# Attention in front of two feed-forward stages: one burst of scores in the last sequence, and normalising taken off GpSimd

## The chip, the cores and the metric

The kernel runs on one core of a Trainium2 chip. The metric is the device time of one execution in microseconds (us), from which comparisons are made over several runs. A core has five engines with instruction queues of their own: PE (TensorE, matrix products into the eight banks of PSUM), DVE (VectorE), ACT (ScalarE), POOL (GpSimd) and SP, which issues loads and stores.

## The reference, cut to what matters

Three stages, all in float32. Attention over 4 sequences of 576 tokens with 8 heads of width 64, a window of 128 tokens and a bias by distance; then a feed-forward stage of width 2048 with a low-rank mixing over tokens; then a gated stage.

```
scores = scale * q @ k^T ;  scores = where(mask, scores + bias, -1e9)
attn   = exp(scores - max) / (sum + 1e-9) ;  x = attn @ v
u = x + (x^T @ U @ V)^T                      # low rank, over tokens
y = u + relu(u @ w_ch1) @ w_ch2              # 512 -> 2048 -> 512
h = relu(y @ w_in) ; ... ; out = (gate) @ w_out
```

The inputs are q, k, v, U, V, w_ch1, w_ch2, w_in, w_spatial, b_spatial and w_out; the output is 4 x 576 x 512.

## The kernel before, in words

Work is written down as tasks (`P.add`, `P.either`) with an engine, a cost in us and what they read and write. A planner (`Plan.run`) then orders all tasks of the whole kernel in list scheduling: it goes forward in time, gives each engine the ready task of the best priority, then sets priorities from the end backward, eight times, and emits the order with the shortest planned time. So a change of one task's engine or cost can move the order of everything up to where the plans meet again. A task given to POOL, or to DVE with `port=True`, also excludes the other of these two in the plan. On the chip each engine runs its instructions in the order emitted and waits by semaphores.

Attention goes by *pairs*: two heads of one sequence, four pairs per sequence, 16 in all. The 576 queries of a pair are nine tiles of 64; tile t needs up to 192 keys. `heads(b, pair)` does:

- L1033, scores: for each tile two matmuls, one per head, in quarters of 64x64 of the PE array, into PSUM tiles named `sc`. `TILES` cuts the nine tiles into six and three, so a pair has one piece of 12 matmul instructions and one of 6 (the trace records each of them as two: 24 and 12). The very first pair has three pieces.
- L1044 on DVE: adds the bias, writes `p`, takes the row maximum (a second small instruction reads it out). L1049 on ACT: exponential with row sums.
- L1055, L1057 on DVE: `rinv`, the inverse of the row sums.
- In sequence 0 (`plain`), L1060 on POOL spreads `rinv` into diagonal blocks `dg` (tiles `y`), L1090 on PE turns these into factors over rows, and L1124 multiplies at the end. In sequences 1 to 3, L1069 on POOL or L1071 on DVE multiplies each tile of `p` by `rinv`; the planner chooses the engine for each tile.
- L1079 on PE: 13 transposes of `p` in four groups (3, 3, 3, 4) into PSUM tiles `at`; L416 (ACT) or L417 (DVE) copies each group out to `ph`.
- L1117 on PE: weighted sums, 32 instructions (64 in the trace); copies to `u`.

`turned` transposes `u` (L1144), and `low_rank` does the mixing (L1160 and L1173 on PE, L1178 on DVE). Weight conversion for the feed-forward stage (L452 on ACT, L458, L459, L462, L465 on DVE, L603 on POOL) runs beside attention, and so do three blocks of 512 tokens of the feed-forward stage: L545 to L547 first layer, L584 to L586 second layer, with L529 (ACT) and L532 (POOL) splitting `u`. These have a later priority and fill PE where attention waits. The next stage on PE starts with L545 on tiles of 384 columns.

PSUM tiles come from rings of banks: `sc` three, `at` three, `acc` one, `f1` one. Sequence 0 uses `acc` and `f1` as well, since nothing else needs them yet. A ring gives its banks in turn, so a new tile waits for the last reader of the bank's former tile.

Of the kernel before, what the change touches and what calls it, by code (L numbers as in the profile page):

```python
# [333 lines left out]
def pool_tt(n):  # L334
    return 0.0021 * n + 0.15
# [3 lines left out]
def tile_kernel(ctx, tc, qT, kT, v, U, V, w1, w2, w_in, wspT, bsp, w_out, bias, out):  # L339
    nc = tc.nc  # L340
# [63 lines left out]
    r_at0 = Ring(in_psum, "at", 3, more=["f1_0"])  # L404
    r_f4 = Ring(in_psum, "at", 3, more=["f1_0"])
    r_a4 = Ring(in_psum, "sc", 3, more=["acc_0"])

    ident = left.tile([128, 128], F32, tag="ident", name="ident")
    make_identity(nc, ident)
# [577 lines left out]
    def heads(b, pair):  # L987
# [1 line left out]
        i = b * H + pair * 2  # L989
        p0 = 10.0 * i  # L990
        hs = slice(pair * 2, pair * 2 + 2)
        sc, tp = (r_sc0, r_at0) if b == 0 else (r_sc, r_at)
        qr, kr = r_qr.new([128, S], F32), r_kr.new([128, S], F32)

        vr = r_vr.new([128, 2, 4, D], F32)
        groups = TILES
        if i:
            for t, src in ((qr, qT), (kr, kT)):
                P.dma(128, S, lambda t=t, src=src: nc.sync.dma_start(out=t.ap(), in_=src[b, hs].rearrange("h d s -> (h d) s")),
# [54 lines left out]
        def rest():  # L1054
# [2 lines left out]
            P.add("DVE", 0.105, lambda: nc.vector.reciprocal(out=rinv[:, sl, :9], in_=rinv[:, sl, :9]), w=[rinv.part(sl)], prio=p0 + 4)  # L1057
            if plain:
                dg = r_d.new([128, 9, D], F32)
                P.add("POOL", pool_tt(S), lambda: nc.gpsimd.tensor_tensor(  # L1060
                    out=dg.ap(), in0=eye.ap().broadcast_to([128, 9, D]),
                    in1=rinv[:, sl, :9].rearrange("p (t o) -> p t o", o=1).broadcast_to([128, 9, D]), op=ALU.mult),
                    r=[rinv.part(sl), eye.part(0), eye.part(1)], w=[dg], prio=p0 + 4)
            else:
                for t in range(9):
                    nk = 64 * min(t + 1, 3)
                    o = lambda t=t, nk=nk: p[:, AT[t] : AT[t] + nk]
                    P.either([
                        ("POOL", pool_tt(nk), lambda o=o, t=t, nk=nk: nc.gpsimd.tensor_tensor(  # L1069
                            out=o(), in0=o(), in1=rinv[:, sl, t : t + 1].broadcast_to([128, nk]), op=ALU.mult)),  # L1070
                        ("DVE", dve2(nk) + 0.06, lambda o=o, t=t: nc.vector.tensor_scalar_mul(  # L1071
                            out=o(), in0=o(), scalar1=rinv[:, sl, t : t + 1])),
                    ], r=[rinv.part(sl)], w=[p.part(t)], prio=p0 + 4 + t / 10, port=True)
# [58 lines left out]
    def turned(b, half):  # L1132

        p0 = 10.0 * (b * H + half * 4 + 3)
        tp = r_at0 if b == 0 else r_at
        xt = r_xt.new([128, 5, 2, 128], F32)
        for c0 in (0, 2, 4):
            cs = range(c0, min(c0 + 2, 5))
            x = tp.new([128, len(cs), 2, 128], F32)
            for i in range(2):  # L1140
                ub = u[b][half * 2 + i]
                for c in cs:

                    P.add("PE", 0.109, lambda x=x, c=c, c0=c0, i=i, ub=ub: nc.tensor.transpose(  # L1144
                        x[:, c - c0, i], ub[:, TOK[c][0] : TOK[c][0] + 128], ident),
                        r=[ub.part(0), ub.part(1)], w=[x], prio=p0 + 8.5)
            copy(engines("h", "ACT"), 256 * len(cs), lambda c0=c0, cs=cs: xt[:, c0 : c0 + len(cs)], x.ap, PSUM,
                 r=[x], w=[xt.part(c0)], prio=p0 + 8.6)
        return xt

    def low_rank(b, xts, pairs, p0):

        sc, tp = (r_sc0, r_at0) if b == 0 else (r_sc, r_at)
        rows = slice(pairs[0] * 32, pairs[-1] * 32 + 32)
        t, th = tp.new([128, 128], F32), r_th.new([128, 128], F32)

        def mix():
            for c in range(5):
                for pair in pairs:
                    nc.tensor.matmul(t[pair * 32 : pair * 32 + 32], u32[:, c], xts[pair // 2][:, c, pair % 2],  # L1160
                                     start=c == 0, stop=c == 4, skip_group_check=True)

        P.add("PE", 5 * 4 * 128 / 2400 + 0.1, mix, r=[u32] + [xts[h].part(c) for h in {p // 2 for p in pairs} for c in (0, 2, 4)],
              w=[t], prio=p0, mode="quarters")
        copy(engines("t", "ACT"), 128, lambda: th[rows], lambda: t[rows], PSUM, r=[t], w=[th], prio=p0 + 0.05)
        for s0 in (0, 288):
            sl = slice(s0, s0 + 288)
            outs = [(sc, tp)[pair % 2].new([128, 288], F32) for pair in pairs]

            def up(sl=sl, outs=outs):  # L1170
                for pair, o in zip(pairs, outs):
                    d = slice(pair * 32, pair * 32 + 32)
                    nc.tensor.matmul(o.ap(), th[d], v32[d, sl], start=True, stop=True)  # L1173

            P.add("PE", 4 * 288 / 2400 + 0.1, up, r=[th] + list(v32.parts.values()), w=outs, prio=p0 + 0.1, mode="quarter rows")
            for pair, o in zip(pairs, outs):
                ub = u[b][pair]
                P.add("DVE", dve(288), lambda o=o, ub=ub, sl=sl: nc.vector.tensor_tensor(  # L1178
                    out=ub[:, sl], in0=o.ap(), in1=ub[:, sl], op=ALU.add),
                    r=[o], w=[ub.part(0), ub.part(1), ub], prio=p0 + 0.2)  # L1180
# [544 lines left out]
```

## Time and profile before

| what | value |
|---|---|
| median of 3 runs | 715.44 us (715.12 to 715.75) |
| the profiled execution | 715.53 us |
| its span, first to last instruction | 713.7 us |
| mean granted TensorE clock | 0.999 |
| PE busy | 700.3 us (98%) |
| DVE busy | 575.2 us (81%) |
| ACT busy | 395.3 us (55%) |
| POOL busy | 68.5 us (10%) |

Attention and what runs beside it fill the first 190 us or so. In the profile busy times come from recorded starts and modelled ends: matmuls are pipelined, so that a matmul of 0.4 us may start 0.23 us after the one ahead of it. The distance of two starts tells more than a duration there. Line numbers below are those of the kernel before; in the changed kernel the same lines stand 1 to 3 further down.

### The profile page before, as it was taken

What the parts mean: (1) busy time and instruction counts of PE and PEld (TensorE: products, weight loads), DVE (VectorE), ACT (ScalarE), POOL (GpSimd) and SP (SyncE); (2) the same over time, 40 slices, a digit from 0 to 9 for tenths busy, and PEclk for the clock granted to TensorE, in tenths of its full rate; (3) what the DMA queues carried; (4) which work ended last, traced back from release to release, by engine and by line L of the source; (5) the groups of instructions that cost most, each with busy time, mean ns of one, the idle gap of its engine ahead of it and who ended that gap; (6) DMA issues with size and microseconds to landing.
All of it is one profiled execution on the core that took longest, in us unless ns stands there. A gap on an engine that the chain in (4) does not pass through costs nothing.

```text
span 713.7 us, 14785 instructions
## 1 busy us (share of the span) xinstructions
PE 700.3 (98%) x5416; PEld 635.7 (89%) x5416; DVE 575.2 (81%) x1641; ACT 395.3 (55%) x1087; POOL 68.5 (10%) x104
## 2 busy tenths in 40 slices
PE   7999999999999999999999999999999999999998
PEld 4767677778799999999999999999999898898896
DVE  5999997775497999999694999697589989859561
ACT  6878576565353745546262563544257566566352
POOL 2142330210400000000000000030010100100000
PEclk9999999999999999999999999999999999999999
DMA  8774212210064165637565455457795202100102
GB/s 258 230 248 148 73 51 83 74 51 2 1 201 158 59 232 204 229 109 244 177 205 194 152 202 192 128 166 240 256 382 181 77 33 68 48 26 1 60 1 75
DMA packets 58798, 98.48 MB, mean 138 GB/s; under 512 B 8356, under 2 KB 38308, under 8 KB 58725
## 3 DMA queue, kind: packets, MB, share of 16 engines
q1 hardware_dynamic: 58437, 97.23, 41.3%
q8 instruction: 43, 0.70, 0.4%
q10 hardware_dynamic: 288, 0.30, 0.1%
q14 instruction: 30, 0.25, 0.1%
HBM read 67.67 MB, written 29.54 MB: 136 GB/s over the span
## 4 chain that ended last, share of the span: by engine, by line
PE 92%; DVE 6%; DMA 1%; issue 1%; ACT 0%; POOL 0%; SPq 0%; DVEq 0%
PE sc L586 8%; PE sc L584 8%; PE sc L585 8%; PE at L885 6%; PE at L886 6%; PE at L887 6%; PE at L1117 4%; PE sc L1033 3%; PE at L1079 3%; PE sc L1412 2%; PE sc L1411 2%; PE sc L1410 2%; PE acc L584 2%; PE at L1412 2%; PE at L1410 2%; PE at L1411 2%
## 5 line engine op out<-in xcount | busy, mean ns | idle before, releaser
L584 PE MATMUL sc<-h,wa 128*128 128x384 f32 (+1 forms) x328 | 110.6, 337 | 0.0
L585 PE MATMUL sc<-h,wa 128*128 128x384 f32 (+1 forms) x328 | 110.5, 337 | 0.0
L586 PE MATMUL sc<-hl,wa 128*128 128x384 f32 x320 | 108.7, 340 | 0.0
L1049 ACT ACTIVATE p<-p,nmax 128x192 f32<-128x192 f32 (+2 forms) x144 | 61.4, 430 | 11.5 <-DVE nmax L1044 11.2
L584 PEld LDWEIGHTS sc<-h,wa 128*128 128x128 f32 x328 | 61.6, 188 | 0.3
L585 PEld LDWEIGHTS sc<-h,wa 128*128 128x128 f32 x328 | 61.5, 187 | 0.3
L885 PE MATMUL at<-xd,wa 128*128 128x384 f32 x180 | 60.9, 338 | 0.0
L886 PE MATMUL at<-xd,wa 128*128 128x384 f32 x180 | 60.8, 338 | 0.0
L887 PE MATMUL at<-xd,wa 128*128 128x384 f32 x180 | 60.8, 338 | 0.0
L586 PEld LDWEIGHTS sc<-hl,wa 128*128 128x128 f32 x320 | 60.1, 188 | 0.0
L933 DVE TENSOR_TENSOR y<-sc,y 128x384 f32<-128x384 f32 (+1 forms) x96 | 40.3, 448 | 20.4 <-PE sc L586 20.2
L1044 DVE CUSTOM_DVE_ANT_0 p<-sc,bias 128x192 f32<-128x192 f32 (+2 forms) x144 | 40.8, 326 | 15.8 <-PE sc L1033 15.6
L905 ACT COPY c<-at 128x384 f32<-128x384 f32 x54 | 25.8, 477 | 42.2 <-PE at L887 42.0
L416 ACT CAST wa<-st 128x256 fp32r<-128x256 f32 (+1 forms) x62 | 27.9, 474 | 26.5 <-DVE st L465 14.2
L897 ACT ACTIVATE h<-c 128x384 fp32r<-128x384 f32 x54 | 28.3, 524 | 19.1 <-DVE c L892 18.9
L1033 PE MATMUL sc<-kr,qr 64*64 64x192 f32 (+2 forms) x576 | 33.3, 328 | 5.3 <-DMA kr<-in_kT 3.3
L892 DVE TENSOR_TENSOR c<-at,c 128x384 f32<-128x384 f32 x54 | 29.7, 551 | 8.3 <-PE at L887 4.7
L885 PEld LDWEIGHTS at<-xd,wa 128*128 128x128 f32 x180 | 33.8, 188 | 0.0
L886 PEld LDWEIGHTS at<-xd,wa 128*128 128x128 f32 x180 | 33.8, 188 | 0.0
L887 PEld LDWEIGHTS at<-xd,wa 128*128 128x128 f32 x180 | 33.8, 188 | 0.0
L1079 PE MATMUL at<-ident,p 128*128 128x128 f32 x208 | 30.9, 284 | 2.5 <-DVE p L1071 1.6
L1079 PEld LDWEIGHTS at<-ident,p 128*128 128x128 f32 x208 | 22.9, 142 | 11.5 <-issue 2.8
(404 smaller groups left out, 1996.5 us busy)
## 6 DMA issues: line engine op xcount, KB each, us to landing
wa<-in_w SPq DMA_DIRECT2D x32, 512.0 KB, 4.4
xd<-formsa SPq DMA_DIRECT2D x24, 192.0 KB, 3.3
qr<-in_qT SPq DMA_DIRECT2D x15, 288.0 KB, 2.9
kr<-in_kT SPq DMA_DIRECT2D x15, 288.0 KB, 3.3
vr<-in_v SPq DMA_DIRECT2D x16, 256.0 KB, 3.3
raw<-in_w_in SPq DMA_DIRECT2D x8, 512.0 KB, 4.0
kepts<-raw SPq DMA_DIRECT2D x14, 288.0 KB, 2.7
out<-h SPq DMA_DIRECT2D x15, 256.0 KB, 2.0
```

The lines of the kernel that those rows point to most:

```text
L584: nc.tensor.matmul(o, wt[:, 0, 0, c], hh[:, j], start=i == 0 and x == 0, stop=False, skip_group_check=True)
L585: nc.tensor.matmul(o, wt[:, 1, 0, c], hh[:, j], start=False, stop=False, skip_group_check=True)
L586: nc.tensor.matmul(o, wt[:, 0, 0, c], hl[:, j], start=False, stop=i == len(wts) - 1, skip_group_check=True)
L885: nc.tensor.matmul(o.ap(), wh()[:, k], xh.ap(), start=start and k == 0, stop=False, skip_group_check=True)
L886: nc.tensor.matmul(o.ap(), wl()[:, k], xh.ap(), start=False, stop=False, skip_group_check=True)
L887: nc.tensor.matmul(o.ap(), wh()[:, k], xl.ap(), start=False, stop=k == 1, skip_group_check=True)
L892: P.add("DVE", dve(N3), lambda: nc.vector.tensor_tensor(out=out.ap(), in0=ps_.ap(), in1=sb.ap(), op=ALU.add), r=[ps_, sb], w=[out], prio=0)
L933: P.add("DVE", dve(m), lambda acc=acc, dst=dst, s=s, m=m, o=o: nc.vector.tensor_tensor(out=dst[:, s : s + m], in0=acc[:, 0, o : o + m], in ...
L1033: nc.tensor.matmul(s[o : o + 64, c0 : c0 + k1 - k0], qr[d, 64 * t : 64 * t + 64], kr[d, k0:k1], start=True, stop=True, skip_group_check=True)
L1044: nc.vector.tensor_tensor_reduce(out=o(), in0=s[:, c0 : c0 + nk], in1=bias_t[:, pair, t % 2, 192 - nk :], scale=-0.125, scalar=BIG, op0=AL ...
L1049: nc.scalar.activation(out=o(), in_=o(), func=AF.Exp, scale=-1.0, bias=nmax[:, sl, t : t + 1], accum_out=sums[:, sl, t : t + 1])
L1079: P.add("PE", 0.109, lambda pt=pt, n_=n_, s0=s0: nc.tensor.transpose(pt[:, n_ - s0], p[:, n_ * 128 : n_ * 128 + 128], ident), r=[p.part(t) ...
```

## The change

A new ring `r_sc1` holds the three `sc` banks and the third `at` bank, and `r_at1` the two `at` banks that are left. The last sequence (b = 3) uses them for scores, transposes, weighted sums, turning and low rank, and issues all nine score tiles of a pair as one task. The diagonals of sequence 0 go from POOL to DVE, and the choice of POOL for the normalising of sequences 1 to 3 is taken away.

```
+    r_sc1 = Ring(in_psum, "sc", 3, more=["at_2"])
+    r_at1 = Ring(in_psum, "at", 2)
...
-        sc, tp = (r_sc0, r_at0) if b == 0 else (r_sc, r_at)
+        sc, tp = (r_sc0, r_at0) if b == 0 else (r_sc1, r_at1) if b >= 3 else (r_sc, r_at)
...
-        groups = TILES
+        groups = [TILES[0] + TILES[1]] if b >= 3 else TILES
...
                 dg = r_d.new([128, 9, D], F32)
-                P.add("POOL", pool_tt(S), lambda: nc.gpsimd.tensor_tensor(
+                P.add("DVE", dve(S), lambda: nc.vector.tensor_tensor(
                     out=dg.ap(), in0=eye.ap().broadcast_to([128, 9, D]),
...
-                    r=[rinv.part(sl), eye.part(0), eye.part(1)], w=[dg], prio=p0 + 4)
+                    r=[rinv.part(sl), eye.part(0), eye.part(1)], w=[dg], port=True, prio=p0 + 4)
...
                     P.either([
-                        ("POOL", pool_tt(nk), lambda o=o, t=t, nk=nk: nc.gpsimd.tensor_tensor(
-                            out=o(), in0=o(), in1=rinv[:, sl, t : t + 1].broadcast_to([128, nk]), op=ALU.mult)),
                         ("DVE", dve2(nk) + 0.06, lambda o=o, t=t: nc.vector.tensor_scalar_mul(
...
 def turned(b, half):
-        tp = r_at0 if b == 0 else r_at
+        tp = r_at0 if b == 0 else r_at1 if b >= 3 else r_at
...
 def low_rank(b, xts, pairs, p0):
-        sc, tp = (r_sc0, r_at0) if b == 0 else (r_sc, r_at)
+        sc, tp = (r_sc0, r_at0) if b == 0 else (r_sc1, r_at1) if b >= 3 else (r_sc, r_at)
```

What this does to the order of instructions is seen at three places. First POOL, from its first work of attention on, before (`y` holds the diagonals, `x` and `wa` are splits of tokens and weights, `p_75` and `p_88` the two buffers of `p`):

```order
L1060 TENSOR_TENSOR y<-eye,rinv 128x576 x4
L532 TENSOR_TENSOR x<-u,x 128x512
L603 TENSOR_TENSOR wa<-st,wa 128x512
L532 TENSOR_TENSOR x<-u,x 128x512 x3
L603 TENSOR_TENSOR wa<-st,wa 128x512 x6
L1069 TENSOR_TENSOR p_88<-p_88,rinv 128x128
L603 TENSOR_TENSOR wa<-st,wa 128x512
L532 TENSOR_TENSOR x<-u,x 128x64 x4
L1069 TENSOR_TENSOR p_75<-p_75,rinv 128x192 x2
```

and in the changed kernel, where L535 and L606 are the former L532 and L603:

```order
L535 TENSOR_TENSOR x<-u,x 128x512
L606 TENSOR_TENSOR wa<-st,wa 128x512
L535 TENSOR_TENSOR x<-u,x 128x512 x3
L606 TENSOR_TENSOR wa<-st,wa 128x512 x7
L535 TENSOR_TENSOR x<-u,x 128x64 x4
```

The four diagonals and all normalising are gone from POOL; the splits keep their order.

Second PE, around the weighted sums of pair 8 (the last pair of sequence 1). Before, from the triple of the second layer ahead of pair 8's transposes to its weighted sums:

```order
L584 MATMUL acc<-h,wa 128x512
L585 MATMUL acc<-h,wa 128x512
L586 MATMUL acc<-h,wa 128x512
L1079 MATMUL at<-ident,p_88 128x128 x13
L1033 MATMUL sc<-kr,qr 64x192 x6
L584 MATMUL acc<-h,wa 128x512
L585 MATMUL acc<-h,wa 128x512
L586 MATMUL acc<-h,wa 128x512
L1117 MATMUL at<-ph,vr 64x64 x30
L1117 MATMUL at<-ph,vl 64x64 x2
```

and in the changed kernel, from the weighted sums of pair 7 to those of pair 8 (L1118, L1080 and L1036 are the former L1117, L1079 and L1033):

```order
L1118 MATMUL at<-ph,vr 64x64 x30
L1118 MATMUL at<-ph,vl 64x64 x2
L1080 MATMUL at<-ident,p_88 128x128 x3
L1036 MATMUL sc<-kr,qr 64x192 x6
L1080 MATMUL at<-ident,p_88 128x128 x10
L1118 MATMUL at<-ph,vr 64x64 x30
L1118 MATMUL at<-ph,vl 64x64 x2
```

The second-layer triples have left this place; the weighted sums of pair 8 follow its transposes at once.

Third PE in the last sequence, before, from the first score piece of pair 14 on (the transposes behind it are pair 13's):

```order
L1033 MATMUL sc<-kr,qr 64x64 x2
L1033 MATMUL sc<-kr,qr 64x128 x2
L1033 MATMUL sc<-kr,qr 64x192 x8
L1079 MATMUL at<-ident,p_75 128x128 x10
L584 MATMUL acc<-h,wa 128x512
L585 MATMUL acc<-h,wa 128x512
L586 MATMUL acc<-h,wa 128x512
L1033 MATMUL sc<-kr,qr 64x192 x6
L584 MATMUL acc<-h,wa 128x512
L585 MATMUL acc<-h,wa 128x512
L586 MATMUL acc<-h,wa 128x512
```

and in the changed kernel, from pair 13's second group of transposes over the scores of pair 14:

```order
L1080 MATMUL at<-ident,p_75 128x128 x3
L1036 MATMUL sc<-kr,qr 64x64 x2
L1036 MATMUL sc<-kr,qr 64x128 x2
L1036 MATMUL sc<-kr,qr 64x192 x14
L587 MATMUL acc<-h,wa 128x512
L588 MATMUL acc<-h,wa 128x512
L589 MATMUL acc<-h,wa 128x512
L1080 MATMUL at<-ident,p_75 128x128 x7
L587 MATMUL acc<-h,wa 128x512
L588 MATMUL acc<-h,wa 128x512
L589 MATMUL acc<-h,wa 128x512
```

The scores of a pair stand together (2 + 2 + 14), and a group of transposes now stands between triples of the second layer.

## Rows read from the trace of the kernel before

**Rows 1.** The page, part 1: busy us, share of the span, instructions.

```profile
PE 700.3 (98%) x5416; PEld 635.7 (89%) x5416; DVE 575.2 (81%) x1641; ACT 395.3 (55%) x1087; POOL 68.5 (10%) x104
```

**Rows 2.** Busy time by stretch; columns as in the first line.

```profile
core 0: us, PE busy (x) PEld busy (x) DVE busy (x) ACT busy (x) POOL busy (x), PEclk, DMA share, GB/s
30.00:40.00 10.00, 9.03 (x139) 6.27 (x133) 9.49 (x37) 8.67 (x29) 3.36 (x3) 1.00 1.05 344
...
70.00:80.00 10.00, 8.86 (x127) 6.54 (x127) 9.48 (x31) 7.47 (x25) 4.27 (x7) 1.00 0.26 84
...
150.00:160.00 10.00, 10.00 (x140) 8.01 (x136) 6.49 (x30) 6.33 (x23) 0.99 (x3) 1.00 0.01 2
```

**Rows 3.** What PE waited for, 0 to 230 us: total, times, longest.

```profile
PE sc L1033 <- DMA kr<-in_kT: 3.3, 1, 3.3
PE sc L1033 <- DMA qr<-in_qT: 1.8, 1, 1.8
PE at L1079 <- DVE p L1071: 1.6, 2, 1.1
```

**Rows 4.** The chain of waits in order of time: start, us, what.

```profile
6.24 2.20 PE sc L1033 x24
...
39.75 2.97 DVE p L1071 x9
...
75.72 2.17 DVE p L1071 x5
```

**Rows 5.** Timeline of PE, four places: start us, us, instruction, count, idle before.

```profile
79.60 0.87 PE L1033 MATMUL sc<-kr,qr 64*64 64x192 f32 x12
...
140.79 1.10 PE L1033 MATMUL sc<-kr,qr 64*64 64x64 f32 x24
141.82 1.31 PE L1079 MATMUL at<-ident,p 128*128 128x128 f32 x10
142.89 0.48 PE L584 MATMUL acc<-h,wa 128*128 128x512 f32 x1
...
143.76 0.87 PE L1033 MATMUL sc<-kr,qr 64*64 64x192 f32 x12
144.56 0.50 PE L584 MATMUL acc<-h,wa 128*128 128x512 f32 x1
...
145.46 1.76 PE L1117 MATMUL at<-ph,vr 128*64 128x64 f32 x60
...
147.27 0.50 PE L584 MATMUL acc<-h,wa 128*128 128x512 f32 x1
...
193.57 0.34 PE L545 MATMUL at<-xd,wa 128*128 128x384 f32 x1
```

**Rows 6.** Timeline of DVE between pair 5's maxima and pair 9's.

```profile
30.51 0.22 DVE L1044 CUSTOM_DVE_ANT_0 p<-sc,bias 128x64 f32<-128x64 f32 x1 [0.96 <-PE sc L1033]
...
39.68 3.05 DVE L1071 TENSOR_SCALAR p<-p,rinv 128x192 f32<-128x192 f32 x9
...
56.49 0.34 DVE L1044 CUSTOM_DVE_ANT_0 p<-sc,bias 128x192 f32<-128x192 f32 x1
...
56.76 0.35 DVE L1044 CUSTOM_DVE_ANT_0 p<-sc,bias 128x192 f32<-128x192 f32 x1
...
58.39 1.28 DVE L462 SCALAR_TENSOR_TENSOR st<-wa,st 128x512 uint32<-128x512 uint32 x2
59.59 0.68 DVE L465 SCALAR_TENSOR_TENSOR st<-wa,st 128x512 uint32<-128x512 uint32 x1
...
66.11 1.40 DVE L1071 TENSOR_SCALAR p<-p,rinv 128x192 f32<-128x192 f32 x6
...
78.67 0.21 DVE L1044 CUSTOM_DVE_ANT_0 p<-sc,bias 128x64 f32<-128x64 f32 x1
```

**Rows 7.** Timeline of POOL beside the nine L1071.

```profile
40.30 1.27 POOL L532 TENSOR_TENSOR x<-u,x 128x512 fp32r<-128x512 f32 x1 [0.45 <-ACT x L529]
```

**Rows 8.** Groups by form on POOL, 0 to 190 us: count, busy us, mean ns, idle before.

```profile
L1060 POOL TENSOR_TENSOR y<-eye,rinv 128x576 f32<-128x576 f32 x4 | 4.6, 1152 | 23.5 <-DVE rinv L1057 17.6 <-DVE u L458 5.8
...
L1069 POOL TENSOR_TENSOR p<-p,rinv 128x192 f32<-128x192 f32 x6 | 3.4, 580 | 21.3 <-PE acc L586 12.8 <-DVE rinv L1057 8.5
```

**Rows 9.** Timeline of DVE: four subtractions of 576 columns and what follows.

```profile
537.51 2.75 DVE L602 TENSOR_TENSOR u<-y,u 128x576 fp32r<-128x576 f32 x4
540.18 0.41 DVE L602 TENSOR_TENSOR x<-h,x 128x256 fp32r<-128x256 f32 x1
```

## The prediction

> A *pair* below is two heads of one sequence; there are 16, numbered 1 to 16 in the order of the loops, and 13 to 16 are those of the last sequence. A *step* is the time from one instruction's start to the next one's start on the same engine, which for pipelined work is what it costs.
>
> **What bounds the kernel now.** I read the page's busy shares first: TensorE 98%, VectorE 81% [rows 1]. Then the stages. In attention (0 to 190 us) the two change places: in 30 to 40 us VectorE is nearly full while TensorE has gaps, in 70 to 80 us both have some, and in 150 to 160 us TensorE is full and VectorE has 3.5 us to spare [rows 2]. The waits of TensorE in attention name one line of compute, 1.6 us on the normalising L1071 [rows 3], and the chain of waits runs through L1071 at 39.75 us and at 75.72 us and otherwise through TensorE [rows 4].
>
> Those 1.6 us understate it, since a matmul's end is modelled and short holes vanish in it. So I priced TensorE's pieces by their steps where it is full [rows 5]: a score piece of 24 matmuls 1.03 us (140.79 to 141.82), one of 12 0.80 us (143.76 to 144.56), ten transposes 1.07 us, a triple of the second layer standing alone 0.87 to 0.90 us, the weighted sums of a pair (64 matmuls of L1117) 1.81 us. The other kinds (first-layer pieces, turning, low rank, row scales) are priced the same way from their own steps, and are as many in both kernels. With the counts from the order of instructions, all of attention's stage sums to 177.9 us: 31 score pieces 29.1, 30 pieces of transposes 23.4, 16 weighted sums 29.0, 144 second-layer matmuls in 30 pieces 38.7, 12 first-layer pieces 34.3, the rest 23.4. Scores start for good at 6.24 us [rows 4], so this work could end at 184.1 us. The next stage starts at 193.57 us [rows 5]: 9.5 us are lost. The same sum up to the score piece that starts at 79.60 us is 63.9 us, so 9.4 of the 9.5 are lost before it. Behind 80 us the stage runs at TensorE's price; before it, VectorE paces it.
>
> VectorE in that stretch: from the first maximum of pair 5 (30.51 us) to the last normalising of pair 8 (the next instruction starts at 78.67 us) it took 48.2 us [rows 6]. Its work by steps (maximum of 192 columns 0.27, weight conversion L462 0.60, normalising 0.23 [rows 6]; copies and additions alike) is 42.6 us. Lost: 5.5 us, about 1.2 idle and 4.3 in instructions held up beside GpSimd. One is visible: nine L1071 took 3.05 us from 39.68 us while GpSimd ran L532 from 40.30 us [rows 6, 7], against 1.40 us for six undisturbed [rows 6].
>
> **The change, part by part.**
>
> *Bursts.* For pairs 13 to 16 a 24-piece and a 12-piece become one piece of 36. The trace has no undisturbed piece of 36. In the shared form the 64x64 quarters work at once, and the longer chain of quarters sets the length: 512 columns in the 24-piece, 384 in the 12-piece, 832 in the burst. From 0.80 and 1.03 us a column costs 1.8 ns and a piece 0.11 us, so a burst costs 1.61 us against 1.83: 0.22 us less. The bounds are 0 (no overlap gained) and 0.36 us. The order has one more place where scores of two pairs now touch, so five times 0.22, -1.1 us. Against it, second-layer work is cut into 35 pieces in place of 30 (0.17 us each, the difference between a triple alone and one that follows another) and transposes into 32 in place of 30: +1.0 us. TensorE's sum goes from 177.9 to 177.8 us. By itself this half is worth -0.1 us (-1.5 to +0.9).
>
> *Two banks less one.* One bank moves from the transposes' ring to the scores' ring, so the four transpose groups, the sums and the turning of pairs 13 to 16 run on two banks. Queued behind a transpose that waits for its bank is everything on TensorE, and ScalarE and VectorE copy the bank out. The order puts a triple (0.87 us) into the break, against 0.47 to 0.60 us of copy. With VectorE 3 us in 10 idle there [rows 2] I take +0.3 us; ends 0 and, if each of the four pairs waits one whole copy, 2.4 us.
>
> *Diagonals.* Four of 1.15 us leave GpSimd [rows 8], and four come to VectorE. Its nearest rows are L602 on 576 columns: four in 2.67 us, 0.67 each [rows 9]. That is +2.7 us on VectorE before 31 us, where it waits for TensorE at the end (0.96 us idle at 30.51 [rows 6]). TensorE waits for a diagonal at the row scales; on VectorE it is shorter but stands in a queue. I take 0, between -0.5 and +0.7 each way.
>
> *Normalising.* Twelve of 108 leave GpSimd (x6 of the large form at 0.58 us [rows 8]) and cost VectorE 12 x 0.22 = 2.6 us. All but the first lay behind 84 us, where TensorE was full, so their going frees nothing.
>
> *Order.* The same planner places everything anew, and here the money lies. Before, four first-layer pieces and four triples lie ahead of the weighted sums of pair 8; in the changed order two and one, with nothing between its transposes and its sums. VectorE gets less weight conversion ahead of pairs 5 to 8, but stays the pacer up to pair 12. I summed VectorE's steps in the changed order from the first maximum of pair 5, which waits for the same TensorE piece as before and so starts at about 30.5 us, to the last copy that a weighted sum needs, and set them against TensorE's own sum plus 6.24 us:
> - pair 8: VectorE 37.3 us of work (43 maxima, 36 normalisings, 18 weight steps, 20 copies and additions, the rest small); TensorE could be there at 63.2 us.
> - pair 9: 53.3 us; TensorE 79.5 us.
> - pair 12: 77.4 us; TensorE 104.6 us.
>
> To VectorE's sums comes what it loses beside GpSimd and in idling. That loss is the unknown. At none, TensorE would lose 4.8 us at pair 8 and the change win 4.7; at the rate of before, 5.5 on 42.6, it is 4.8, 6.9 and 10. GpSimd's long operations that caused it (L532, L603) stay, eight of them by pair 8, twelve by pair 9, and few long ones after, so I take 3.9, 5.6 and 7.0. With 0.2 us from copy to matmul TensorE is there at 71.9, 89.6 and 115.1 us: 8.7, 10.1 and 10.5 us lost. From pair 13 VectorE's sum lies over 6 us ahead, and nothing more is lost to it.
>
> The rule that bears on this: the row shows a doubled L1071 beside a GpSimd operation [rows 6, 7]. The Trainium skill (Advanced Engine Details and Errata, VectorE Performance Modes) says that VectorE's second SBUF port is shared with GpSimd, so that GpSimd and VectorE's two-port forms block each other. By that rule taking sixteen operations off GpSimd also gives VectorE back what they blocked; the trace agrees in kind, but only 2.4 us of such steps lie beside L1069, all behind 80 us, and the sum on TensorE stays as it is.
>
> *Sum.* Lost 10.5 in place of 9.5: +1.0. Pieces -0.1, two banks +0.3. Together +1.2 us. What follows attention has the same order on TensorE, and its first matmul still has triples ahead of it (9 in place of 11, some 1.4 us less cover), which I cost at nothing; loads are issued in another order too, and after the first scores TensorE waited for none [rows 3]. On the profiled execution (715.53 us, span 713.7) that is 716.7 us; the runs' median, 715.44, is 0.1 lower, and I leave it at 716.7.
>
> **Rivals.**
> - *VectorE keeps losing at its old rate up to pair 12.* For it: the changed order leaves VectorE no slack for longer, so each hold-up lands on TensorE. Against: the long GpSimd operations are over by then. It decides from a loss above 8 us by pair 12; at 10 us TensorE loses 13.5: +4.0 - 0.1 + 0.3, 719.7 us. Slower.
> - *VectorE loses little.* For it: sixteen GpSimd operations are gone and hold-ups are chance meetings. At half the rate (2.4, 3.5, 5.0) pair 12 loses 8.5 and pair 9 8.0; with bursts at their better end (-0.7 more) that is -1.0 - 0.8, 713.7 us. Faster.
> - *The early half does nothing, and only the pieces count.* The new order moves waiting from one pair to another and loses the same 9.5: -0.1 + 0.3, 715.7 us. No change. For it: both orders are TensorE-bound at their end.
>
> **How the numbers follow.** A difference under 0.2% (1.4 us) can't be told from none here. Forecast 0.45, old rate 0.23, little loss 0.20, nothing 0.12. The forecast's own range is 715.2 to 718.2, and about half of it lies above the bound (716.9): slower 0.23 + 0.20 = 0.43, same 0.25 + 0.12 = 0.37, faster 0.20. The range for all of it, 713.6 to 719.4 us, leaves out the upper part of the old-rate case and the lower tail of the little-loss case.
>
> **What would show it.** Right: the maxima of pair 5 start near 30.5 us; L1117 of pair 8 near 72 us and of pair 12 near 115 us, released by VectorE's copies; the next stage starts near 194.8 us; the burst of 36 takes about 1.6 us; no gap on TensorE within pairs 13 to 16 above 0.3 us. Wrong: if the weighted sums of pair 8 come before 70 us, VectorE lost less and the kernel is faster; if those of pair 12 come after 118 us, it is the first rival; and a burst of 1.8 us would take back its part.

## The result and the profile after

The changed kernel takes 722.25 us (median of six runs, 720.97 to 726.54) against 715.60 us for the kernel before on the same chip (six runs, 715.12 to 716.36): a ratio of 1.010, 95% interval 1.0086 to 1.0114. The forecast was 716.7 us with a range up to 719.4. The side that had the most chance, slower, came true; the size lies outside the range.

The profiled execution took 721.52 us with a span of 718.8 us (713.7 before); it is one of the faster of the six, whose spans run from 718.8 to 724.8 us. Busy times hardly moved [rows 1]. Page, part 1, of the kernel after:

```profile
PE 700.5 (97%) x5416; PEld 638.7 (89%) x5416; DVE 580.4 (81%) x1657; ACT 397.3 (55%) x1086; POOL 60.9 (8%) x89
```

What changed is where TensorE waits. Windows of the kernel after, columns as in [rows 2]:

```profile
40.00:50.00 10.00, 7.70 (x87) 5.50 (x89) 9.56 (x22) 5.27 (x11) 5.66 (x5) 0.84 0.29 95
70.00:80.00 10.00, 7.84 (x163) 6.36 (x163) 9.79 (x35) 7.50 (x27) 2.02 (x2) 1.00 0.46 145
90.00:100.00 10.00, 7.73 (x143) 6.06 (x143) 9.77 (x43) 7.34 (x28) 6.01 (x9) 1.00 0.20 60
150.00:160.00 10.00, 9.96 (x135) 7.67 (x134) 6.80 (x35) 6.21 (x23) 0.26 (x2) 1.00 0.06 20
```

TensorE loses over 2 us in each of the first three windows of 10 us, and in each of these VectorE is 95% busy or more. At 150 us, in the last sequence with its burst, nothing is lost. The waits of TensorE behind the first scores, 0 to 230 us, after [rows 3]:

```profile
PE at L1080 <- DVE u L1179: 2.6, 1, 2.6
PE at L1118 <- ACT p L1052: 1.8, 1, 1.8
PE sc L1174 <- DVE th L420: 1.7, 1, 1.7
PE sc L1036 <- DVE nmax L1047: 0.8, 1, 0.8
PE at L1080 <- DVE p L1072: 0.6, 1, 0.6
```

Three single waits make 6.1 us. (The engine named is the profile's inference. For the wait of 1.8 us the exponential named had ended some 0.7 us before; the rows below show another releaser.) The answer stands in VectorE's timeline at those places, beside GpSimd's. First VectorE after [rows 6]:

```profile
31.45 0.75 DVE L1063 TENSOR_TENSOR y<-eye,rinv 128x576 f32<-128x576 f32 x1
32.11 0.22 DVE L1047 CUSTOM_DVE_ANT_0 p<-sc,bias 128x64 f32<-128x64 f32 x1
...
39.78 4.62 DVE L1072 TENSOR_SCALAR p<-p,rinv 128x192 f32<-128x192 f32 x8
44.44 0.29 DVE L420 COPY th<-at 64x128 f32<-64x128 f32 x1
...
47.86 1.77 DVE L465 SCALAR_TENSOR_TENSOR st<-wa,st 128x512 uint32<-128x512 uint32 x1
...
62.01 0.35 DVE L1047 CUSTOM_DVE_ANT_0 p<-sc,bias 128x192 f32<-128x192 f32 x1
...
62.28 1.00 DVE L1058 TENSOR_SCALAR rinv<-sums 128x9 f32<-128x9 f32 x1
...
74.61 1.70 DVE L465 SCALAR_TENSOR_TENSOR st<-wa,st 128x512 uint32<-128x512 uint32 x1
76.23 0.55 DVE L420 COPY ph<-at 128x384 f32<-128x384 f32 x1
76.70 0.34 DVE L1047 CUSTOM_DVE_ANT_0 p<-sc,bias 128x192 f32<-128x192 f32 x1
...
78.45 0.16 DVE L1058 TENSOR_SCALAR rinv<-sums 128x9 f32<-128x9 f32 x1
...
81.79 0.69 DVE L465 SCALAR_TENSOR_TENSOR st<-wa,st 128x512 uint32<-128x512 uint32 x1
...
85.48 1.16 DVE L468 SCALAR_TENSOR_TENSOR st<-wa,st 128x512 uint32<-128x512 uint32 x1
...
87.89 3.96 DVE L1072 TENSOR_SCALAR p<-p,rinv 128x64 f32<-128x64 f32 x7
91.77 0.44 DVE L1179 TENSOR_TENSOR u<-at,u 128x288 f32<-128x288 f32 x1
```

and GpSimd after, the splits beside them [rows 7]:

```profile
39.41 1.27 POOL L535 TENSOR_TENSOR x<-u,x 128x512 fp32r<-128x512 f32 x1 [36.88 <-ACT x L532]
40.89 1.28 POOL L606 TENSOR_TENSOR wa<-st,wa 128x512 fp32r<-128x512 f32 x1 [0.21 <-ACT wa L419]
42.97 1.31 POOL L535 TENSOR_TENSOR x<-u,x 128x512 fp32r<-128x512 f32 x1 [0.81 <-ACT x L532]
47.61 3.15 POOL L535 TENSOR_TENSOR x<-u,x 128x512 fp32r<-128x512 f32 x2 [3.32 <-ACT x L532]
61.98 2.53 POOL L606 TENSOR_TENSOR wa<-st,wa 128x512 fp32r<-128x512 f32 x2 [11.22 <-ACT wa L419]
74.49 1.27 POOL L606 TENSOR_TENSOR wa<-st,wa 128x512 fp32r<-128x512 f32 x1 [9.98 <-DMA vr<-in_v]
...
87.40 2.95 POOL L606 TENSOR_TENSOR wa<-st,wa 128x512 fp32r<-128x512 f32 x2 [1.31 <-ACT wa L419]
```

Set a row against the same work undisturbed, and the difference is a *hold-up*. Eight normalisings take 1.88 us alone (below) and took 4.62; L465, the former L462, takes 0.69 us at 81.79 and took 1.77 and 1.70; L1058 on nine numbers takes 0.16 us at 78.45 and took 1.00, until the split that began at 61.98 us was over (1.28 us later). Counted so for each instruction (its duration less that of its undisturbed form, where it exceeds 0.15 us), 30 to 120 us hold 8.3 us in nine instructions after, and 4.4 us in nine before. A maximum, which reads PSUM, runs unharmed beside the same split (62.01 us, 0.35). The Trainium skill (SBUF — State Buffer, "SBUF: two separate sides") says that GpSimd and those VectorE operations that run in a two-port mode or have two SBUF inputs share a port pair, and that whichever starts first has it for its whole instruction. The rows at 62 us agree; a row further down (92.28 us, 1.90) outlasts any single instruction of GpSimd, which the page's rule alone does not give.

TensorE's timeline after shows who pays [rows 5]:

```profile
44.78 0.51 PE L1174 MATMUL sc<-v,th 32*128 32x288 f32 x1 [1.70 <-DVE th L420]
...
46.95 1.99 PE L1036 MATMUL sc<-kr,qr 64*64 64x64 f32 x24
48.86 2.38 PE L1118 MATMUL at<-ph,vr 128*64 128x64 f32 x60
...
76.88 1.76 PE L1118 MATMUL at<-ph,vr 128*64 128x64 f32 x60 [1.76 <-ACT p L1052]
...
92.27 0.55 PE L1080 MATMUL at<-ident,p 128*128 128x128 f32 x3 [2.58 <-DVE u L1179]
...
121.38 1.76 PE L1118 MATMUL at<-ph,vr 128*64 128x64 f32 x60
...
125.89 1.63 PE L1036 MATMUL sc<-kr,qr 64*64 64x64 f32 x36
127.45 0.50 PE L548 MATMUL f<-x,wa 128*128 128x512 f32 x1
...
198.58 0.34 PE L548 MATMUL at<-xd,wa 128*128 128x384 f32 x1
```

At 44.78 us the low rank's second product waits for `th`, whose copy stood on VectorE behind the eight normalisings. At 76.88 the weighted sums of pair 8 wait for the last copy of their transposes to `ph`, which stood on VectorE behind L465 until 76.23 and ended at 76.78. At 92.27 the transposes of pair 9 wait for a bank that the addition at 91.77 empties, and this stood behind seven normalisings. Behind the first wait TensorE also ran slower, as windows of 1 us show:

```profile
44.00:45.00 1.00, 0.22 (x2) 0.22 (x4) 0.94 (x3) 0.00 (x0) 0.29 (x1) 1.00 0.00 0
...
47.00:48.00 1.00, 1.00 (x19) 1.00 (x22) 1.00 (x4) 1.00 (x4) 0.39 (x1) 0.50 0.00 0
```

The granted clock is 0.50, the level of 1.2 GHz, from 47 to 50 us; the score piece of 24 takes 1.91 us (46.95 to 48.86), against 1.03 in [rows 5].

### The profile page after: what moved, and what is told of

Same layout as the page of the kernel before. It is cut to its first block, busy times and chain, and to the rows that moved or that the text cites. A ratio compares the mean times of both kernels' runs of the same rounds, so it can differ in the third digit from the quotient of the medians.

```text
span 718.8 us, 14760 instructions
## 1 busy us (share of the span) xinstructions
PE 700.5 (97%) x5416; PEld 638.7 (89%) x5416; DVE 580.4 (81%) x1657; ACT 397.3 (55%) x1086; POOL 60.9 (8%) x89
## 4 chain that ended last, share of the span: by engine, by line
PE 91%; DVE 5%; ACT 2%; DMA 1%; issue 1%; SPq 0%
PE sc L589 8%; PE sc L587 8%; PE sc L588 8%; PE at L888 6%; PE at L889 6%; PE at L890 6%; PE at L1118 3%; PE sc L1036 3%; PE at L1080 3%; PE sc L1413 2%; PE sc L1411 2%; PE sc L1412 2%; DVE p L1072 2%; PE at L1413 2%; PE at L1412 2%; PE at L1411 2%
## 5 line engine op out<-in xcount | busy, mean ns | idle before, releaser
L1047 DVE CUSTOM_DVE_ANT_0 p<-sc,bias 128x192 f32<-128x192 f32 (+2 forms) x144 | 40.8, 325 | 10.5 <-PE sc L1036 10.5
L1036 PE MATMUL sc<-kr,qr 64*64 64x192 f32 (+2 forms) x576 | 33.8, 340 | 6.0 <-DMA kr<-in_kT 3.3
L1080 PEld LDWEIGHTS at<-ident,p 128*128 128x128 f32 x208 | 23.8, 144 | 13.2 <-DVE u L1179 3.5
L1080 PE MATMUL at<-ident,p 128*128 128x128 f32 x208 | 31.4, 286 | 4.0 <-DVE u L1179 2.6
```

Source lines behind the costliest of these rows:

```text
L1036: nc.tensor.matmul(s[o : o + 64, c0 : c0 + k1 - k0], qr[d, 64 * t : 64 * t + 64], kr[d, k0:k1], start=True, stop=True, skip_group_check=True)
L1047: nc.vector.tensor_tensor_reduce(out=o(), in0=s[:, c0 : c0 + nk], in1=bias_t[:, pair, t % 2, 192 - nk :], scale=-0.125, scalar=BIG, op0=AL ...
L1080: P.add("PE", 0.109, lambda pt=pt, n_=n_, s0=s0: nc.tensor.transpose(pt[:, n_ - s0], p[:, n_ * 128 : n_ * 128 + 128], ident), r=[p.part(t) ...
```

## The experiments

Times are medians; "before" ran beside each group at 715.6 to 716.0 us. Theory A: the new order puts more of VectorE's instructions beside GpSimd's 512-column splits, at places TensorE waits for. Rival B: the extra 5.3 us of VectorE's work. Rival C: one queue place and the clock behind it. Rival D: two banks too few.

**VectorE's extra work in the old order.** Planner costs as before; only what is emitted changes (the normalising likewise):

```
-                P.add("POOL", pool_tt(S), lambda: nc.gpsimd.tensor_tensor(
+                P.add("POOL", pool_tt(S), lambda: nc.vector.tensor_tensor(
                     out=dg.ap(), in0=eye.ap().broadcast_to([128, 9, D]),
```

> The kernel before, with its planner untouched, so that every engine has the order of before; only the four diagonals and the twelve normalisings that GpSimd did are done by VectorE at the same places (20 of some 1450 rows of VectorE's order differ). VectorE gets the full 5.3 us of extra work, TensorE, ScalarE and the loads keep their order. Theory A (the loss comes from the new order, which puts more of VectorE's instructions beside GpSimd's 512-column splits, at places TensorE waits for): 715.0 to 717.0 us. Rival B (VectorE's extra work itself, in a stretch where VectorE is full): 719 to 722 us.

716.78 us, ratio 1.0017 (1.0007 to 1.0027). With all the extra work and the old order the price is about 1.2 us. B falls as the main cause: in the old order VectorE's extra work costs some 1 us, as A expected.

**GpSimd's splits cut short.** The order is untouched on TensorE, VectorE, ScalarE and SP. The splits of weights are cut as shown, those of tokens (L535) in the same way; the products beside attention then read the high part where the low part stood, so this kernel leaves the low parts out:

```
+            P.add("POOL", pool_tt(k * c), lambda: nc.gpsimd.tensor_tensor(
+                out=b[:, 1, :1, :64], in0=st[:, :1, :64], in1=f32(b[:, 0, :1, :64]), op=ALU.subtract),
...
-            nc.tensor.matmul(o, wt[:, 1, k], a[ia], start=False, stop=False)
+            nc.tensor.matmul(o, wt[:, 0, k], a[ia], start=False, stop=False)
```

> The changed kernel in its own order on TensorE, VectorE, ScalarE and SP; only GpSimd's 512-column splits of tokens and weights beside attention are cut to 64 columns, and the first and second layer beside attention read the high part where the low part stood (this leaves the low parts of those products out). Instructions beside GpSimd can be held up by 0.1 to 0.2 us at most. Theory A: the 8.3 us of hold-ups on VectorE go, of which 4 to 6 us lie on the path: 716 to 718.5 us. Rival B: the work of VectorE is as much as before, 721 to 722.5 us.

> The control to the run with short splits: the same cut in the kernel before (low parts of the products beside attention left out), its own order kept. Theory A: the 4.1 us of hold-ups before 80 us go, 1.5 to 4 us on the path: 712 to 714 us, so that the two kernels with short splits lie within 1 to 4.5 us of each other (6.6 with long ones). Rival B: 715 to 716 us, and the distance of the two stays at 6 us or more.

The changed kernel falls to 711.80 us (ratio 0.9952, 0.9938 to 0.9965), 10.5 us less; the one before to 713.71 (0.9975, 0.9966 to 0.9985), 1.9 us less. No hold-up is left in the first. So without GpSimd's length the changed order is the *better* one by 1.9 us; A had expected it still behind by 1 to 4.5, and 716 to 718.5 us where 711.80 came: it made too little of the hold-ups. VectorE, TensorE at pair 12's sums and at the next stage, in the changed kernel with short splits:

```profile
39.55 1.88 DVE L1078 TENSOR_SCALAR p<-p,rinv 128x192 f32<-128x192 f32 x8
...
114.53 0.69 PE L1124 MATMUL at<-ph,vr 128*64 128x64 f32 x16
...
191.18 0.34 PE L554 MATMUL at<-xd,wa 128*128 128x384 f32 x1
```

The eight normalisings take 1.88 us in place of 4.62, and the next stage starts 7.4 us sooner than after. The spans of these two traces also lie 7.4 us apart (711.4 and 718.8), less than the medians' 10.5: the traced execution of the change is one of its faster ones, that with short splits (714.24 us) the slowest of its seven. Full length again, low parts still unread:

> A control to the run with short splits: GpSimd's splits have their full 512 columns again, in the changed kernel's order, but the first and second layer beside attention still read the high part where the low part stood (the low parts of those products are left out). Theory A (what GpSimd's length does to VectorE): the time of the changed kernel, 720 to 725 us, with about 8 us of hold-ups. Rival E (TensorE waits for the split itself, unseen): 712 to 716 us, as with short splits.

722.63 us (1.0103, 1.0087 to 1.0120), the change's own time: the length does it, not a wait for the splits' results, and not the parts left out.

**Which splits.** The same edit, but the first five keep 512 columns, or (with `> 5`) all others:

```
+                count[0] += 1
+                if count[0] <= 5:
+                    nc.gpsimd.tensor_tensor(out=b[:, 1], in0=st.ap(), in1=f32(b[:, 0]), op=ALU.subtract)
```

> As the run with short splits, but the first five splits of GpSimd (38 to 51 us in the changed kernel's trace) have their 512 columns, the later ones 64 (low parts left out as there). Theory A, with the hold-ups adding up: four hold-ups of 4.3 us come back, 715 to 718 us. Theory C (TensorE's idle time at 44.8 us and the lower granted clock behind it make most of the loss): 719 us or more, with a granted clock under 0.9 from 40 to 50 us.

> The complement: the first five splits of GpSimd are cut to 64 columns, the seven of weights from 62 to 90 us keep 512 (low parts left out as there). Theory A: five hold-ups of 4.4 us come back, 714 to 717 us, and the gains of the two complements against the changed kernel add up to some 10 us. Theory C: 713 us or less.

716.95 us (ratio 1.0012, 1.0001 to 1.0023) and 718.32 (1.0039, 1.0027 to 1.0052): 5.2 and 6.5 us above the run with none, together 11.7 against 10.5 for all. They add up, as A had it, though the late ones cost 1.3 us more than it allowed. One row each, early and late:

```profile
38.85 4.63 DVE L1086 TENSOR_SCALAR p<-p,rinv 128x192 f32<-128x192 f32 x8
```

```profile
82.85 3.94 DVE L1086 TENSOR_SCALAR p<-p,rinv 128x64 f32<-128x64 f32 x7
```

4.63 us here, 4.62 in the change, 3.94 and 3.96: the hold-ups come back in the same instructions at the same length, from other kernels' starts. The traces of the next two kernels, which keep the change's order, hold the same nine instructions again, 8.3 us in each. The hold-ups are set by the order, not met by chance.

**One queue place, and the clock.** Two kernels in the change's order: one with the three copies of `th` on ScalarE, one with 14 transposes that run inside the wait:

```
-        copy(engines("t", "ACT"), 128, lambda: th[rows], lambda: t[rows], PSUM, ...
+        P.either([("ACT", act(128, 0.06), lambda: nc.scalar.copy(out=th[rows], in_=t[rows])),
+                  ("DVE", dve(128), lambda: nc.scalar.copy(out=th[rows], in_=t[rows]))], ...
...
+                for _ in range(14 if b == 0 and len(pairs) == 2 and pairs[0] == 2 and not sl.start else 0):
+                    nc.tensor.transpose(outs[0][:, :128], ident, ident)
```

> The changed kernel in its own order; only the three copies of the low rank's result (th) that the planner gave to VectorE go to ScalarE at the same place in the order. At 44.8 us TensorE waited 1.7 us for one of them, which stood behind held-up normalisings on VectorE, and then ran its next 2.7 us at a lower granted clock. Theory C (this one queue place and the clock behind it carry much of the loss): 718.5 to 720 us, the wait of 1.7 us gone and the granted clock of 40 to 50 us at 1.00. Theory A: the next instruction of TensorE that needs VectorE waits in its place, 720.8 to 722.5 us.

> The changed kernel, complete and in its own order, with 14 transposes of the identity (some 1.5 us, results overwritten) put ahead of the second low-rank product, where TensorE waited 1.7 us at 44.8 us; they run inside the wait. Theory C (the clock): the granted clock of 40 to 50 us stays at 1.00, the score piece behind takes 1.03 us in place of 1.92 and the weighted sums 1.81 in place of 2.36, and the time falls by 1.5 us or more, to 718 to 720.7 us. Theory A: VectorE paces this stretch whatever TensorE's clock is, 721.5 to 724 us.

The first gave 725.09 us (1.0125, 1.0089 to 1.0161; four runs, 720.0 to 725.96), the second 721.44 (1.0082, 1.0055 to 1.0109; four, 719.14 to 723.69). The first lies above both ranges of its expectation, the second above C's and 0.1 us under A's. In the first the wait of 1.7 us went, and the granted clock of 40 to 50 us was 0.85 all the same, since it had fallen to 0.50 by 40 us, behind an earlier wait. In the second it stayed at 1.00; its TensorE:

```profile
42.30 1.69 PE L1173 MATMUL sc<-ident 128*128 128x128 f32 x14
44.18 0.51 PE L1176 MATMUL sc<-v,th 32*128 32x288 f32 x1 [0.18 <-DVE th L420]
...
46.32 1.10 PE L1036 MATMUL sc<-kr,qr 64*64 64x64 f32 x24
...
51.90 1.09 PE L1036 MATMUL sc<-kr,qr 64*64 64x128 f32 x20 [1.00 <-DVE nmax L1047]
52.91 0.50 PE L548 MATMUL f<-x,wa 128*128 128x512 f32 x1
```

The score piece took 1.03 us (46.32 to 47.35), yet the next pair's piece waited for VectorE again. From the first scores, L548 came 46.9 us later (6.00 to 52.91), against 47.6 after (6.30 to 53.94): of 1.4 us gained (0.9 in the piece, 0.5 in the sums) 0.7 were kept. Nor did the clock stay up elsewhere:

```profile
70.00:80.00 10.00, 8.02 (x142) 6.57 (x138) 8.77 (x31) 6.71 (x23) 2.54 (x2) 0.83 0.45 142
```

C falls as the main cause, but the clock has a share. The filled kernel has the change's hold-ups (8.3 us in its trace), and its four runs lie in the order of their mean granted clock: 719.14 us at 1.000, 720.58 at 0.998, 722.31 at 0.995, 723.69 at 0.993. The run at 1.000 is 7.3 us above the 711.80 of the kernel with short splits and 3.1 us below the change's 722.25. So, as an estimate from one run that has no trace, some 7 of the 10.5 us are waiting and some 3 the lower clock. In the kernel with long late splits the three runs at a mean granted clock of 1.000 took 715.4, 716.0 and 716.9 us, the five at 0.995 718.5 to 719.6. The change's own runs had 0.986 to 0.998, the kernel before 0.999 to 1.000 and the one with short splits 1.000 in all seven, so in this order the lower clock too comes with the hold-ups. Not every order pays for it: VectorE alone (next) took 717.57 us at 1.000 and 717.40 to 718.12 at 0.995.

**The halves, each planned anew.** Rings and burst alone, and VectorE alone (their lines of the diff above), with splits long and short:

> One half of the change: diagonals and normalising on VectorE alone, with the rings and the score pieces of before; the planner places everything anew, its order is neither that of before nor that of the changed kernel (212 and 297 of some 3470 rows of TensorE differ). Rival B (VectorE's work is the cost): 719 to 723 us. Theory A (the order's meetings with GpSimd's 512-column splits are the cost, whichever edit makes the order): between 713 and 722 us, in step with the hold-ups on VectorE from 30 to 100 us in its own trace, 4 us of them for a time near 715.7 and 8 us for one near 721.

> The other half: the burst of nine score tiles and the rings of four and two banks in the last sequence, GpSimd keeping its diagonals and its part of the normalising; planned anew. Rival D (the two rings cost something in the last sequence): waits of TensorE in pairs 13 to 16 and 717 us or more. Theory A: the same rule as for the other half, 713 to 722 us in step with the hold-ups on VectorE up to 100 us. Rival B: 715 to 716 us, as VectorE has no more work than before.

> Diagonals and normalising on VectorE alone in that half's own order, splits cut to 64 columns (low parts of the products beside attention left out). If VectorE's extra work of 5.3 us costs something by itself, this order is slower without hold-ups too: 714.5 us or more against 713.7 us of before with short splits. If only hold-ups cost: 711 to 714 us. By A1 the 7.5 us of hold-ups would be worth 9 us: 708 to 709.5 us.

> The burst alone in its own order, GpSimd's 512-column splits beside attention cut to 64 columns (the low parts of the products beside attention left out); GpSimd keeps its part of the normalising. Theory A1 (a hold-up costs what it delays on the path, whichever the order): 6.9 us of hold-ups at the rate of the changed kernel (10.5 us for 8.3) go, 706.5 to 709 us. Theory A2 (the price depends on how much of it the order covers; near the rate of before, 1.9 us for 4.1): 711 to 713.5 us.

| kernel | hold-ups 30 to 120 us | long splits, us | ratio (95%) | short splits, us | difference |
|---|---|---|---|---|---|
| before | 4.4 | 715.6 | | 713.71 | 1.9 |
| burst alone | 6.9 | 715.61 | 1.0003 (0.9992 to 1.0014) | 712.86 | 2.8 |
| VectorE alone | 7.5 | 717.49 | 1.0034 (1.0021 to 1.0047) | 713.35 | 4.1 |
| both | 8.3 | 722.25 | 1.0100 (1.0086 to 1.0114) | 711.80 | 10.5 |

The halves cost 0.0 and 1.9 us, both together 6.65. By the rule in their expectations (4 us of hold-ups for 715.7 us, 8 for 721) the burst would have taken some 719.5 us and VectorE alone 720.3: A missed both. With short splits none of the three is slower than the kernel before, so VectorE's extra work is covered in the new orders. The first two rows keep 0.8 and 1.2 us of hold-ups there, beside GpSimd's own normalising. A1, one price for every hold-up, falls: a microsecond of hold-up that goes is worth about 0.5, 0.5, 0.55 and 1.26 us. (Taken from the ratios, each against the kernel before beside it, the differences are 1.8, 3.1, 5.1 and 10.6 us, and the finding is the same; by the spans of the traces, one execution each, they are 1.6, 2.6, 2.8 and 7.4.) Which instructions are held decides, and for whom. In "both" the rows show three places where TensorE's next instruction waits for the held one or for what stands behind it on VectorE, and the order has nothing else for TensorE there; that these alone raise the price is read from the rows and was not tried. D falls: the burst alone costs nothing.

**Ways out.** Four splits of 128 columns in place of one of 512; then ScalarE as a further choice for the normalising, planned anew:

```
+                    for q in range(0, m, 128 if packed else m):
+                        e = min(128 if packed else m, m - q)
+                        nc.gpsimd.tensor_tensor(
+                            out=tl[il][:, o + q : o + q + e], in0=ub[:, s + q : s + q + e],
...
+                        ("ACT", act(nk, 0.09, 1), lambda o=o, t=t: nc.scalar.activation(
+                            out=o(), in_=o(), func=AF.Copy, scale=rinv[:, sl, t : t + 1])),
```

> The changed kernel, complete and in its own order on TensorE, VectorE, ScalarE and SP; each of GpSimd's 512-column splits beside attention becomes four of 128 columns one behind the other. The time of one split rises from 1.28 us to some 1.5 to 1.7 us, but an instruction of VectorE that meets one can be held for no longer than one fourth, some 0.4 us. Theory A: hold-ups fall from 8.3 us to 2 to 4 us and the time to 713.5 to 718 us, nearer to the run with short splits (711.8) than to the change (722.3). If GpSimd holds VectorE for as long as it has work queued, not for one instruction: 721 to 724 us.

> The same fourths in the kernel before, own order kept. Theory A: hold-ups before 80 us fall from 4.1 us to 1 to 2 us, the time to 713.5 to 715.5 us (the run with short splits gave 713.7). If GpSimd holds VectorE for as long as it has work queued: 715.5 to 717 us.

> The changed kernel, complete, with ScalarE as a second choice for each normalising (a copy scaled by the inverse of the row sums); the planner places everything anew. It takes work off VectorE, the pacer up to 120 us, and puts it on ScalarE, which is busy for 50 to 97% of that stretch. If VectorE's work and hold-ups pace: 712 to 718 us. If ScalarE becomes the next pacer, since exponentials queue behind normalisings there: 719 to 724 us.

> The burst alone, complete, with ScalarE as a third choice for each normalising beside VectorE and GpSimd, planned anew. If VectorE paces up to 120 us and ScalarE has room: 710 to 714.5 us, faster than both kernels. If ScalarE becomes the pacer: 715.5 to 719 us.

Fourths in the changed kernel: 716.95 us (1.0020, 1.0006 to 1.0033), 5.3 us won back, with 5.7 us of hold-ups still there (2 to 4 expected). In the kernel before: 716.52 (1.0015, 1.0005 to 1.0025), a little *slower*, against A; its hold-ups, counted the same way, rose from 4.4 us in nine instructions to some 5.5 in 25, most of them of 0.2 us. In the changed kernel 18 of the 19 that are left are of 0.2 to 0.3 us, but a hold-up is not limited to one fourth, as the last shows, with GpSimd beside it:

```profile
92.28 1.90 DVE L1069 TENSOR_SCALAR rinv<-sums 128x9 f32<-128x9 f32 x1
```

```profile
90.78 3.37 POOL L545 TENSOR_TENSOR x<-u,x 128x64 fp32r<-128x64 f32 x9
```

It ended at 94.2 us with the nine pieces (of 64 or 128 columns, none longer than 0.47 us) that stood in line on GpSimd, five of which began behind it.

ScalarE as a choice brings the complete change to 715.21 us (0.9992, 0.9982 to 1.0002), and the burst alone to 712.60 (0.9957, 0.9944 to 0.9970): faster than both kernels. There ScalarE takes 49 of the 108 normalisings, hold-ups of 30 to 120 us are 3.2 us, and its group of the large form, 0 to 190 us, reads (count, busy us, mean ns, idle before):

```profile
L1074 ACT ACTIVATE p<-p,rinv 128x192 f32<-128x192 f32 x42 | 16.6, 447 | 4.5 <-DVE rinv L1060 2.9 <-DVE nmax L1047 1.4
```

One costs ScalarE 447 ns, dearer than VectorE's 0.23 us step [rows 6], but ScalarE was not the pacer, and none of its 49 took over 0.47 us, so no split held one up. Both of these kernels are planned anew, so part of the gain may be the order's; that was not taken apart.

## Why the prediction was wrong

*What bounds.* Right in the main, and so is the side: the change lost time because VectorE, full, made TensorE wait early. VectorE paced it up to pair 9; from pair 9's sums (96.75 us) to pair 12's TensorE took 24.63 us for 25.1 priced and lost nothing more. Two readings were too mild. The chain of waits of the kernel before lies on VectorE in all its longer pieces from 30.74 to 54.93 us, not only at L1071. And among the nine L1071 one took 1.32 us where 0.31 is usual: not doubled but held for a whole split.

*The step that failed* is "GpSimd's long operations that caused it (L532, L603) stay, eight of them by pair 8, twelve by pair 9, and few long ones after, so I take 3.9, 5.6 and 7.0". From the first maximum of pair 5 (32.11 us), 37.3 us of work and 0.2 us to the matmul, pair 8's sums at 76.88 lost 7.3 us where the forecast had 3.9; by the same sum with 77.4, pair 12's at 121.38 lost 11.7 where it had 7.0. With short splits the sums at 114.53 us (first maximum at 31.89) lost 5.0. So 5.0 us go without any hold-up (VectorE idles 3.4 us of them in that trace; its work was priced about 1 us too low), and 6.7 more come from 8.3 us of hold-ups. The forecast had 7.0 for both together, from a rate per us of work and a count of GpSimd's operations; the rate belongs to an order. The little-loss rival called hold-ups "chance meetings", and the forecast's rate treats them so too: but the same ones come back from run to run of an order, and could have been looked for there, where VectorE's work from SBUF to SBUF stands next to a split whose ScalarE copy has just ended.

*The start.* Pair 5's maxima began at 32.11, not 30.5. Some 1 us is no effect of the change: the score piece at 9.72 us ran at the longer steps that the kernel before showed only up to 9.44 us. The old order shows them too in other traces, with short splits (9.47 us, 1.91 in place of 1.03) and with VectorE's extra work, and the change's order with `th` moved does not (8.84 us, 1.04). Why they last longer in some executions is open; the granted clock was 1.00. With VectorE's extra work:

```profile
9.52 1.99 PE L1033 MATMUL sc<-kr,qr 64*64 64x64 f32 x24
```

*Diagonals.* Four at 0.67 us, as priced (31.45 to 32.11, 0.66).

*Bursts.* 125.89 to 127.45: 1.56 us against 1.61. *Pieces* (-0.1) were mis-sized: from pair 12's sums to the next stage took 77.2 us where the sum had 79.4, so the change wins 2.2 us more there than I gave it; the 36 second-layer triples there took 27.6 us for 28.9 priced, since a triple between other pieces cost less than one alone had. *Two banks* (+0.3): about nothing.

*The sum* comes out so: start 1.6 later, 4.7 more lost by pair 12, 2.5 won behind it: 198.58 us for the next stage in place of 194.8. Of what is then missing to 722.25, 0.9 us lie outside the span of the traced execution (2.7 around it, 1.8 before), and 0.7 are the distance from that execution to the median. Two measures of the text fell on the rival's side: "those of pair 12 come after 118 us" (121.38) and a loss above 8 us. *The first rival*, VectorE losing at its old rate, was the right one, with 719.7 us still too low: it had neither a rate as high as this order's nor TensorE's lower clock, which no term held.

*What stays open:* how exactly the 10.5 us divide between waiting and the lower clock, since the 7 and 3 above rest on one run at a mean clock of 1.000 that has no trace; and why the two halves together cost more than their sum, beyond the three places read in the rows.

## What to carry to other kernels

When a planner re-orders a full engine, price its hold-ups from the new order, pair by pair with the neighbour it blocks, and not by the old order's rate. A test that shortens the blocker and leaves every order alone shows whether an order is bad or only blocked, with a second run at full length for what the shortening leaves out. Offer work taken off a pacing engine to one that the blocker does not hold up and that has room: with ScalarE as a choice at 447 ns the burst took 712.60 us, without it 715.61.

## What the runs showed of the hardware

- An instruction of VectorE on nine numbers per partition took 1.00 us beside a split of 512 columns, and 1.90 us where nine of 64 or 128 stood in line: a small instruction is held about as long as a large one (L465 lost 1.0 to 1.1 us), and the hold-up can outlast one instruction of GpSimd.
- GpSimd is slowed as well: its split took 1.27 us where VectorE was the one held (74.49 us), and 1.93 us beside conversions that VectorE ran on with:

```profile
84.15 1.93 POOL L606 TENSOR_TENSOR wa<-st,wa 128x512 fp32r<-128x512 f32 x1 [3.35 <-ACT wa L419]
```

- In the trace of the change TensorE's granted clock was still 1.00 while TensorE waited (0.22 busy from 44 to 45 us) and 0.50, the level of 1.2 GHz, when it was full again (1.00 busy from 47 to 48). Runs of one kernel lay some 3 to 5 us apart with their mean granted clock in the orders named above, and not at all in another.
